# Attention of batches 1 to 3 in three TensorE bursts a job instead of five, and a new order of the banded products

## The chip, the cores and the metric

The kernel runs on one core of a Trainium2 chip. A core has a matrix engine (TensorE, with its own queue), VectorE (DVE), ScalarE (ACT), GpSimd (POOL) and SyncE (SP), which here only issues DMA transfers. Each engine works through its own instructions in order, and semaphores tie the engines together. The metric is the time of one execution on the device, in microseconds (us); a run's time is one execution, and the median of the runs counts.

## The reference

Four batches, 8 heads, 576 positions, head dimension 64. Attention has two branches that are added: one over keys and values that are averaged in groups of four (144 queries by 144 keys, each result repeated four times), and one in which a position sees only the seven positions within three of it. The result goes through two gated feed-forward layers.

```
q_d, k_d, v_d = means of q, k, v over groups of 4 positions
out_up    = repeat(softmax(scale * q_d @ k_d.T) @ v_d, 4)
mask      = abs(pos[:, None] - pos[None, :]) < 4
out_local = softmax(where(mask, scale * q @ k.T, -1e9)) @ v
x = (out_up + out_local), heads side by side: 2304 x 512
x = ((sigmoid(x @ w_gate) * (x @ w_val)) @ w_out)        # 512 -> 1536 -> 512
h = x @ w_in                                              # 512 -> 2048
out = (h * sigmoid(1.702 * h)) @ w_out2                   # 2048 -> 512
```

## The kernel before

**Dense layers.** Every dense product is done in single precision by three passes over a split into high and low halves: high by high, low by high, high by low (L822 to L824, function `passes`). A pass is a 128x128 weight times 512 columns. Hidden values go to the PSUM banks `ph`, results to the banks `acc`. Layer 1 is done batch by batch; a *visit* of a batch is 432 passes. The weights arrive as 64-bit words; ScalarE (L744) and VectorE (L746, L748, L753) turn them into 32-bit numbers, ScalarE makes the high half `whi` (L762), VectorE or GpSimd the low half `wlo` (L764). In the visit of batch 0, when the weights come for the first time, the low halves are VectorE's.

**Attention.** It is cut into 16 jobs: a job is a batch and a pair of heads. The four jobs of batch 0 run before the dense work; those of batch b+1 run within the visit of batch b, in bursts on TensorE between dense passes. A job before has five bursts:

- `scores` (L570): banded scores of 24 query tiles by two heads, on 64x32 parts of the array, into two banks `pa`. VectorE adds the mask (L577), then softmax on VectorE and ScalarE (L585 to L596), and VectorE transposes the probabilities into `tt` (L597).
- `down` (L610): pooled scores of 144 by 144, into two banks. VectorE finds the maxima (L617, L620), ScalarE takes the exponential, VectorE the sum's reciprocal (L632, L633), ScalarE scales: `pd`.
- `down_t` (L654): eight transposes of `pd`, copied by ScalarE into `pdt`.
- `values`, first part: the first half of the banded values (`band(0)`, L682, on 32x64 parts) and the pooled values (L690). ScalarE copies the pooled part to `up`.
- `values`, second part: `band(1)`, again L682.

Then `combine` adds `up` to the bands out of the banks (three reads on VectorE, L711), and ScalarE and VectorE split the sum into the halves `xhi` and `xlo` (L720 for the low half), which are the dense layer's input in the next visit. L507 on VectorE pools the values `vg`; GpSimd pools queries and keys (L538, L540 into `qd`, `kd`).

**Order.** All operations are given to a planner (`Plan`) with an estimated duration, the buffers that they read and write, and a due time; for attention that is a fraction of the job's stretch (`due(x)`). The planner runs through time, gives each engine the ready operation with the smallest due time, and writes the fixed order that each engine then executes. A buffer or bank is held from its first writer to its last reader. Batches 1 to 3 have only two banks (`pas`) for attention, so each burst must wait until the readers of the burst before have let them go; batch 0 has more. At the start, filler products (L1272) stand where TensorE would have nothing to do.

## Time and profile before

| what | value |
|---|---|
| median of 3 runs | 942.98 us (941.73 to 944.8) |
| the profiled execution's own time | 942.11 us |
| its span in the trace | 940.4 us |
| granted TensorE clock, mean of the span | 0.992 |
| TensorE busy | 922.7 us, 98 % |
| TensorE weight loads busy | 761.4 us, 81 % |
| VectorE, ScalarE, GpSimd busy | 685.8, 499.7, 364.2 us |

The profiled execution is one of its own beside the three runs; durations in the trace are its. A share of busy time is an average over stages: attention of batch 0 with the start, the visits of layer 1, then layer 2. TensorE's entries in a timeline carry a modelled end, so one reads their starts: a dense pass is shown with 0.39 us but its successor starts 0.227 us later. A burst is one row with a count of hardware passes (a single-precision product is two of them), and its effect is seen in the starts of the dense passes around it.

### The profile page before, as it was taken

Reading aid. Unit: us, or ns where it says so; the run is one execution under the profiler, and the core shown is the slowest. Engines: PE = TensorE matmul, PEld = TensorE weight load, DVE = VectorE, ACT = ScalarE, POOL = GpSimd, SP = SyncE. Lnnn points to the kernel's source line nnn. Section 1 sums busy time; section 2 is a strip of 40 time slices with the busy share of each in tenths; the row PEclk is TensorE's granted clock in tenths of the full one; section 3 lists DMA queues with packets and bytes.
Section 4 is the critical chain, followed back from the end, with each engine's and each line's share of the span. In section 5 each row is a group of like instructions: output and inputs, shape, how many; then the busy total and the mean of one; then the engine's idle time right before and its main releaser. Section 6 shows DMA issues by size and latency. Waiting matters only on the chain.

```text
span 940.4 us, 19224 instructions
## 1 busy us (share of the span) xinstructions
PE 922.7 (98%) x7515; PEld 761.4 (81%) x7515; DVE 685.8 (73%) x1170; ACT 499.7 (53%) x1080; POOL 364.2 (39%) x337
## 2 busy tenths in 40 slices
PE   6999999999999999999999999999999999999997
PEld 5777777877778778789988888888888788888896
DVE  5799999887767786755565639878897977764364
ACT  3666666455554555555655436545664544554463
POOL 6352202334233442234678423222696222232241
PEclk8899999999999999999999999999999999999999
DMA  9447647463265633220154103011551101043000
GB/s 274 138 152 205 206 136 196 138 175 135 71 177 181 174 127 102 84 75 2 62 184 153 51 0 135 23 45 41 181 166 46 62 24 45 33 149 110 30 16 23
DMA packets 51980, 101.70 MB, mean 108 GB/s; under 512 B 5489, under 2 KB 18619, under 8 KB 51890
## 3 DMA queue, kind: packets, MB, share of 16 engines
q1 hardware_dynamic: 51890, 100.48, 34.4%
q8 instruction: 59, 0.97, 0.4%
q14 instruction: 31, 0.25, 0.1%
HBM read 75.29 MB, written 25.17 MB: 107 GB/s over the span
## 4 chain that ended last, share of the span: by engine, by line
PE 88%; DVE 6%; DMA 2%; ACT 1%; issue 1%; SPq 1%; POOL 0%; ACTq 0%; DVEq 0%
PE ph L822 14%; PE ph L823 13%; PE ph L824 13%; PE acc L822 9%; PE acc L823 9%; PE acc L824 9%; PE pa L822 5%; PE pa L824 5%; PE pa L823 5%; PE pa L682 2%; DMA vt<-v 1%; PE pa L570 1%; DMA vg<-v 1%; PE acc L494 1%; PE pa L690 1%; DVE we L748 1%
## 5 line engine op out<-in xcount | busy, mean ns | idle before, releaser
L764 POOL TENSOR_TENSOR wlo<-w,whi 128x512 fp32r<-128x512 f32 x77 | 104.9, 1362 | 179.9 <-ACT whi L762 177.9
L822 PE MATMUL ph<-xhi,whi 128*128 128x512 f32 (+1 forms) x418 | 166.3, 398 | 0.4 <-ACT th L865 0.4
L824 PE MATMUL ph<-xlo,whi 128*128 128x512 f32 (+1 forms) x418 | 161.5, 386 | 1.4 <-POOL xlo L720 1.4
L823 PE MATMUL ph<-xhi,wlo 128*128 128x512 f32 (+1 forms) x418 | 161.7, 387 | 0.0
L762 ACT CAST whi<-w 128x512 fp32r<-128x512 f32 x159 | 97.9, 619 | 83.5 <-PE ph L824 28.2
L764 POOL TENSOR_TENSOR wlo<-wr,whi 128x512 fp32r<-128x512 f32 x58 | 78.9, 1361 | 142.7 <-ACT whi L762 133.0
L822 PEld LDWEIGHTS ph<-xhi,whi 128*128 128x128 f32 x418 | 78.6, 188 | 19.9 <-issue 4.3
L824 PEld LDWEIGHTS ph<-xlo,whi 128*128 128x128 f32 x418 | 78.7, 188 | 18.3 <-POOL xlo L720 2.2
L823 PEld LDWEIGHTS ph<-xhi,wlo 128*128 128x128 f32 x418 | 78.7, 188 | 14.5 <-DVE wlo L764 0.4
L822 PE MATMUL acc<-ghi,whi 128*128 128x512 f32 (+1 forms) x240 | 90.3, 376 | 0.0
L870 DVE SCALAR_TENSOR_TENSOR th<-th,ph 128x512 f32<-128x512 f32 (+1 forms) x68 | 41.2, 605 | 66.8 <-PE ph L824 59.3
L762 ACT CAST whi<-wr 128x512 fp32r<-128x512 f32 (+1 forms) x115 | 67.1, 587 | 40.3 <-PE ph L824 13.7
L823 PE MATMUL acc<-ghi,wlo 128*128 128x512 f32 (+1 forms) x240 | 88.4, 369 | 0.0
L824 PE MATMUL acc<-glo,whi 128*128 128x512 f32 (+1 forms) x240 | 88.3, 368 | 0.0
L764 DVE TENSOR_TENSOR wlo<-w,whi 128x512 fp32r<-128x512 f32 x82 | 62.8, 766 | 23.3 <-ACT whi L762 23.2
L865 ACT ACTIVATE th<-ph 128x512 f32<-128x512 f32 (+1 forms) x68 | 36.3, 534 | 48.0 <-PE ph L824 48.0
L744 ACT ACTIVATE we<-w 128x512 f32<-128x512 f32 x68 | 45.7, 672 | 19.0 <-DMA w<-w 13.5
L748 DVE SCALAR_TENSOR_TENSOR we<-w,we 128x512 int32<-128x512 int32 x68 | 55.0, 808 | 1.1
L538 POOL TENSOR_TENSOR half<-qt 128x288 f32<-128x288 f32 x16 | 20.2, 1265 | 85.1 <-DMA qt<-qT 84.8
L822 PEld LDWEIGHTS acc<-ghi,whi 128*128 128x128 f32 x240 | 45.2, 189 | 7.9 <-issue 0.6
L824 PEld LDWEIGHTS acc<-glo,whi 128*128 128x128 f32 x240 | 45.3, 189 | 7.6
L874 DVE TENSOR_TENSOR glo<-th,ghi 128x512 fp32r<-128x512 f32 (+1 forms) x60 | 46.5, 776 | 6.6 <-ACT ghi L873 5.8
(254 smaller groups left out, 2289.1 us busy)
## 6 DMA issues: line engine op xcount, KB each, us to landing
w<-w SPq DMA_DIRECT2D x68, 512.0 KB
w<-gd SPq DMA_DIRECT2D x32, 256.0 KB
gd<-w SPq DMA_DIRECT2D x30, 256.0 KB
w2d<-we SPq DMA_DIRECT2D x28, 256.0 KB
qt<-qT SPq DMA_DIRECT2D x16, 288.0 KB
kt<-kT SPq DMA_DIRECT2D x16, 288.0 KB
st<-x2d SPq DMA_DIRECT2D x36, 128.0 KB
x2d<-ev SPq DMA_DIRECT2D x16, 256.0 KB
```

Source lines behind the costliest of these rows:

```text
L538: op("pool", 760.0, lambda: nc.gpsimd.tensor_add(half.t, s[:, :, :, 0], s[:, :, :, 1]), [bsrc], [half], due)
L682: nc.tensor.matmul(s.t[h * D:(h + 1) * D, q:q + NQ], vt.t[ks, g, v0 + h * D:v0 + (h + 1) * D], tt.t[ks, h, g, :NQ], start=True, stop=True, ...
L744: op("act", 617.0, lambda: nc.scalar.activation(e.t.bitcast(F32), words(1, F32), AF.Copy, scale=2.0 ** -112), [w], [e], due)
L748: op("dve", 602.0, lambda: nc.vector.scalar_tensor_tensor(e.t, words(0), 29, e.t, op0=ALU.logical_shift_right, op1=ALU.bitwise_or), [w], [ ...
L762: op("act", act_ns(n), lambda: nc.scalar.copy(vh(), vm()), [rm], [rh], due)
L764: op(eng, ns, lambda: on.tensor_sub(vl(), vm(), vh().bitcast(F32)), [rm, rh], [rl], due)
L822: nc.tensor.matmul(o, lhi, rhi, start=first, stop=False, skip_group_check=more)
L823: nc.tensor.matmul(o, llo, rhi, start=False, stop=False, skip_group_check=more)
L824: nc.tensor.matmul(o, lhi, rlo, start=False, stop=last, skip_group_check=more)
L865: op("act", act_ns(n, True), lambda h=h: nc.scalar.activation(th.t[:, :n], h.t[:, :n], AF.Tanh, scale=0.5 if layer == 1 else 1.702 / 4.0), ...
L870: op("dve", dve_ns(n), lambda: nc.vector.scalar_tensor_tensor(th.t[:, :n], th.t[:, :n], 1.0, hb[-1].t[:, :n], op0=ALU.add, op1=ALU.mult), ...
L874: op("dve", dve_ns(n), lambda: nc.vector.tensor_sub(gl.t[:, :n], th.t[:, :n], gh.t[:, :n].bitcast(F32)), [th, gh], [gl], t)
```

## The change

For batches 1 to 3 a job has three bursts. The first holds the banded scores (now L571) and the pooled scores (L618), in the same two banks, the pooled ones behind the column where the banded ones end. The second holds the first half of the bands (L693) and the transposes (L676). The third holds the second half of the bands (L693) and the pooled values (L716). Second and third share one pair of banks, so that a job takes a pair twice instead of four times. The due times move: pooled scores from 0.5 to 0.1 of the stretch, transposes from 0.65 to 0.5, values from 0.9 to 0.6, combine from 0.9 and 1.0 to 0.6 and 0.7. Batch 0 keeps its bursts. For all batches the loop of a band now has the head outside and the two row quarters inside, so that the quarter, and the bank with it, changes at every product, and the planned durations of the values are smaller.

```diff
--- before.py
+++ after.py
@@ -542,7 +542,7 @@
 
         def front(self):
 
-            return [self.pools, self.scores, self.down]
+            return [self.pools, self.scores, self.down] if self.b == 0 else [self.pools, self.scores]
 
         def back(self):
             return [self.down_t, self.values]
@@ -560,8 +560,9 @@
 
             ss = [bank(self.banks) for _ in range(2)]
             qt, kt, sc, pt, tt, nm, sm = self.qt, self.kt, self.sc, self.pt, self.tt, self.nm, self.sm
-
-            def pe():
+            n = NG * NU
+
+            def scored():
                 for t in range(NT):
                     g, i = divmod(t, 4)
                     t = NG * i + g
@@ -571,12 +572,24 @@
                                          qt.t[hs, NQ * t:NQ * t + 32], kt.t[hs, NQ * t:NQ * t + NU],
                                          start=True, stop=True, tile_position=(h * D, 32 * i))
 
-            n = NG * NU
-            op("pe", 1500.0, pe, [qt, kt], [*ss, (sc, 0), (sc, 1)], self.due(0.1))
+            when = self.due(0.1)
+            if self.b == 0:
+                op("pe", 1500.0, scored, [qt, kt], [*ss, (sc, 0), (sc, 1)], when)
+            else:
+                qd, kd, nmd, smd, pd = self.qd, self.kd, self.nmd, self.smd, self.pd
+
+                def pe():
+                    scored()
+                    self.pooled(ss, n)
+
+                op("pe", 1600.0, pe, [qt, kt, qd, kd],
+                   [*ss, (sc, 0), (sc, 1), nmd, (smd, 0), (smd, 1), (pd, 0), (pd, 1)], when)
             for h in range(2):
                 op("dve", dve_ns(n), lambda h=h: nc.vector.tensor_add(
                     sc.t[:, h], ss[h].t[:, :n].rearrange("p (g c) -> p g c", c=NU), mask),
-                   [ss[h]], [(sc, h)], self.due(0.1))
+                   [ss[h]], [(sc, h)], when)
+            if self.b:
+                self.pooled_softmax(ss, n, when, [(sc, 0), (sc, 1)])
 
             def spread(x):
                 return x.t[:, :, :, None].to_broadcast([P, 2, NG, NU])
@@ -598,31 +611,37 @@
                 out=tt.t.rearrange("p h g c -> p (h g c)"), in_=pt.t.rearrange("p h g c -> p (h g c)")),
                [pt], [tt], at)
 
+        def pooled(self, ss, c):
+            qd, kd = self.qd, self.kd
+            for r in range(2):
+                for h in range(2):
+                    nc.tensor.matmul(ss[h].t[:GH, c + r * G:c + (r + 1) * G],
+                                     qd.t[h * D:(h + 1) * D, r * GH:(r + 1) * GH],
+                                     kd.t[h * D:(h + 1) * D, :], start=True, stop=True)
+
         def down(self):
 
 
             ss = [bank(self.banks) for _ in range(2)]
             qd, kd, nmd, smd, pd = self.qd, self.kd, self.nmd, self.smd, self.pd
-
-            def pe():
-                for r in range(2):
-                    for h in range(2):
-                        nc.tensor.matmul(ss[h].t[:GH, r * G:(r + 1) * G],
-                                         qd.t[h * D:(h + 1) * D, r * GH:(r + 1) * GH],
-                                         kd.t[h * D:(h + 1) * D, :], start=True, stop=True)
-
             at = self.due(0.5)
-            op("pe", 560.0, pe, [qd, kd], [*ss, nmd, (smd, 0), (smd, 1), (pd, 0), (pd, 1)], at)
+            op("pe", 560.0, lambda: self.pooled(ss, 0), [qd, kd],
+               [*ss, nmd, (smd, 0), (smd, 1), (pd, 0), (pd, 1)], at)
+            self.pooled_softmax(ss, 0, at, [])
+
+        def pooled_softmax(self, ss, c, at, masked):
+
+            nmd, smd, pd = self.nmd, self.smd, self.pd
             for h in range(2):
                 op("dve", dve_ns(2 * G), lambda h=h: nc.vector.reduce_max(
-                    nmd.t[:, 2 * h:2 * h + 2], ss[h].t[:GH, :2 * G].rearrange("p (r k) -> p r k", k=G), axis=AX.X),
-                   [ss[h]], [(nmd, h)], at)
-            op("dve", 90.0, lambda: nc.vector.tensor_scalar_mul(nmd.t, nmd.t, -SCALE_D), [], [nmd], at)
+                    nmd.t[:, 2 * h:2 * h + 2], ss[h].t[:GH, c:c + 2 * G].rearrange("p (r k) -> p r k", k=G),
+                    axis=AX.X), [ss[h]], [(nmd, h)], at)
+            op("dve", 90.0, lambda: nc.vector.tensor_scalar_mul(nmd.t, nmd.t, -SCALE_D), masked, [nmd], at)
 
             def ex(h):
                 for r in range(2):
                     x = 2 * h + r
-                    nc.scalar.activation(pd.t[:, h, r], ss[h].t[:GH, r * G:(r + 1) * G], AF.Exp,
+                    nc.scalar.activation(pd.t[:, h, r], ss[h].t[:GH, c + r * G:c + (r + 1) * G], AF.Exp,
                                          bias=nmd.t[:, x:x + 1], scale=SCALE_D, accum_out=smd.t[:, x:x + 1])
 
             for h in range(2):
@@ -643,29 +662,45 @@
 
         def down_t(self):
             self.pdt = buf("pdt")
-            ss = [bank(self.banks) for _ in range(2)]
+            ss = self.ss = [bank(self.banks) for _ in range(2)]
             pd, pdt = self.pd, self.pdt
+            c, due, more = (0, 0.65, []) if self.b == 0 else (HALF // 2, 0.5, [halves[self.b, self.hp // 2].vt, self.tt])
 
             def pe():
+                if self.b:
+                    self.band(0, *ss)
                 for h in range(2):
                     for kh in range(2):
                         for r in range(2):
-                            o = kh * G + r * GH
+                            o = c + kh * G + r * GH
                             nc.tensor.transpose(ss[h].t[:GH, o:o + GH], pd.t[:, h, r, kh * GH:(kh + 1) * GH],
                                                 ident.t[:GH, :GH])
 
-            op("pe", 500.0, pe, [(pd, 0), (pd, 1), ident], [*ss, (pdt, 0), (pdt, 1)], self.due(0.65))
+            op("pe", 500.0 + 500.0 * len(more) / 2, pe, [(pd, 0), (pd, 1), ident, *more],
+               [*ss, (pdt, 0), (pdt, 1)], self.due(due))
             for h in range(2):
                 op("act", 370.0, lambda h=h: nc.scalar.copy(
-                    pdt.t[:, h], ss[h].t[:GH, :2 * G].rearrange("p (k q) -> p k q", q=G)),
-                   [ss[h]], [(pdt, h)], self.due(0.65))
+                    pdt.t[:, h], ss[h].t[:GH, c:c + 2 * G].rearrange("p (k q) -> p k q", q=G)),
+                   [ss[h]], [(pdt, h)], self.due(due))
+
+        def band(self, x, sa, sz):
+
+            vt, tt, v0 = halves[self.b, self.hp // 2].vt, self.tt, self.hp % 2 * P
+            for g in range(NG):
+                for h in range(2):
+                    for s, i in ((sa, x), (sz, 2 + x)):
+                        ks, q = slice(32 * i, 32 * i + NU), NQ * (NG * x + g)
+                        nc.tensor.matmul(s.t[h * D:(h + 1) * D, q:q + NQ],
+                                         vt.t[ks, g, v0 + h * D:v0 + (h + 1) * D], tt.t[ks, h, g, :NQ],
+                                         start=True, stop=True, tile_position=(32 * i, h * D))
 
         def values(self):
 
 
 
             b, hp = self.b, self.hp
-            sa, sz = (bank(self.banks) for _ in range(2))
+            early = self.b > 0
+            sa, sz = self.ss if early else (bank(self.banks) for _ in range(2))
             half = halves[b, hp // 2]
             vd, vt, pdt, tt = half.vd, half.vt, self.pdt, self.tt
             up = self.up = buf("up")
@@ -674,17 +709,8 @@
                 new_x((1, b))
             xh, xl = xs[1, b]
 
-            def band(x):
-                for g in range(NG):
-                    for s, i in ((sa, x), (sz, 2 + x)):
-                        ks, q = slice(32 * i, 32 * i + NU), NQ * (NG * x + g)
-                        for h in range(2):
-                            nc.tensor.matmul(s.t[h * D:(h + 1) * D, q:q + NQ],
-                                             vt.t[ks, g, v0 + h * D:v0 + (h + 1) * D], tt.t[ks, h, g, :NQ],
-                                             start=True, stop=True, tile_position=(32 * i, h * D))
-
             def pe():
-                band(0)
+                self.band(int(early), sa, sz)
                 for kh in range(2):
                     for h in range(2):
                         nc.tensor.matmul(sa.t[h * D:(h + 1) * D, c0:c0 + G],
@@ -693,10 +719,12 @@
 
 
             xfs = [buf("xf") for _ in range(2)]
-            op("pe", 1400.0, pe, [vd, pdt, vt, tt], [sa, sz, up, *xfs], self.due(0.9))
+            at = self.due(0.6 if early else 0.9)
+            op("pe", 1100.0, pe, [vd, pdt, vt, tt], [sa, sz, up, *xfs], at)
             op("act", 260.0, lambda: nc.scalar.activation(up.t, sa.t[:, c0:c0 + G], AF.Copy, scale=0.25),
-               [sa], [up], self.due(0.9))
-            op("pe", 700.0, lambda: band(1), [vt, tt, up], [sa, sz], self.due(0.9))
+               [sa], [up], at)
+            if not early:
+                op("pe", 500.0, lambda: self.band(1, sa, sz), [vt, tt, up], [sa, sz], at)
             for n, s in enumerate((sa, sz)):
                 self.combine(n * HALF, (n + 1) * HALF, s, xfs[n], n == 0, xh, xl)
 
@@ -704,7 +732,7 @@
             b, hp, up = self.b, self.hp, self.up
             hi = min(z, T)
             m = hi - a
-            at = self.due(0.9 if first else 1.0)
+            at = self.due((0.9 if first else 1.0) - (0.3 if b else 0.0))
             part = (hp, first)
 
             def add(out, o0, o1):
```

TensorE, job 0 of batch 2, end of the banded scores (`kt_123`, `qt_121` are its keys and queries, `pa_156` and `pa_157` the two banks, `acc`, `ph` banks of dense passes). Before, two pieces that have 56 dense passes between them:

```order
L570 MATMUL pa_156<-kt_123,qt_121 32x30
L570 MATMUL pa_157<-kt_123,qt_121 32x30
L822 MATMUL acc_151<-ghi_94,whi_79 128x512
L823 MATMUL acc_151<-ghi_94,wlo_83 128x512
L824 MATMUL acc_151<-glo_96,whi_79 128x512
```

```order
L824 MATMUL ph_155<-xlo_92,whi_80 128x512
L610 MATMUL pa_156<-kd_134,qd_132 72x144
L610 MATMUL pa_157<-kd_134,qd_132 72x144
L610 MATMUL pa_156<-kd_134,qd_132 72x144
L610 MATMUL pa_157<-kd_134,qd_132 72x144
L822 MATMUL ph_155<-xhi_90,whi_80 128x512
```

After, one piece:

```order
L571 MATMUL pa_156<-kt_123,qt_121 32x30
L571 MATMUL pa_157<-kt_123,qt_121 32x30
L618 MATMUL pa_156<-kd_134,qd_132 72x144
L618 MATMUL pa_157<-kd_134,qd_132 72x144
L618 MATMUL pa_156<-kd_134,qd_132 72x144
L618 MATMUL pa_157<-kd_134,qd_132 72x144
L850 MATMUL acc_151<-ghi_94,whi_79 128x512
L851 MATMUL acc_151<-ghi_94,wlo_83 128x512
```

The pooled scores moved forward by 60 dense passes, and the two places at which the dense passes were left are one.

TensorE, the same job's transposes (`pd_138` are the pooled probabilities, `tt_128` the banded ones). Before:

```order
L824 MATMUL ph_154<-xlo_92,whi_78 128x512
L654 MATMUL pa_156<-ident,pd_138 72x72 x4
L654 MATMUL pa_157<-ident,pd_138 72x72 x4
L822 MATMUL ph_154<-xhi_90,whi_78 128x512
L823 MATMUL ph_154<-xhi_90,wlo_82 128x512
```

After:

```order
L693 MATMUL pa_156<-tt_128,vt 64x24
L693 MATMUL pa_157<-tt_128,vt 64x24
L676 MATMUL pa_156<-ident,pd_138 72x72 x4
L676 MATMUL pa_157<-ident,pd_138 72x72 x4
L850 MATMUL ph_155<-xhi_90,whi_80 128x512
L851 MATMUL ph_155<-xhi_90,wlo_84 128x512
```

The transposes come 27 dense passes earlier and directly behind the first half of the bands, which itself comes 57 passes earlier than it did.

VectorE, job 1 of batch 1, in the visit of batch 0 (`xf_145`, `xf_146` take the sums out of the two banks; `small`, `pt_126`, `tt_128` belong to the softmax of job 2; `w`, `we`, `wlo` to the dense weights). Before:

```order
L597 STREAM_TRANSPOSE tt_128<-pt_126 128x384
L711 TENSOR_TENSOR xf_145<-pa_156,up_143 128x288
L746 TENSOR_SCALAR we_87<-we_87 128x512
L874 TENSOR_TENSOR glo_95<-th_97,ghi_93 128x512
L720 TENSOR_TENSOR xlo_92<-xf_145,xhi_90 128x288
L748 SCALAR_TENSOR_TENSOR we_87<-w_86,we_87 128x512
L711 TENSOR_TENSOR xf_146<-pa_157,up_143 128x224
L753 SCALAR_TENSOR_TENSOR w_114<-w_86,we_87 128x512
L711 TENSOR_TENSOR tails<-pa_157,up_143 128x64
```

After:

```order
L602 TENSOR_REDUCE small<-pt_126 128x12
L774 TENSOR_SCALAR we_88<-we_88 128x512
L739 TENSOR_TENSOR xf_145<-pa_156,up_143 128x288
L739 TENSOR_TENSOR xf_146<-pa_157,up_143 128x224
L739 TENSOR_TENSOR tails<-pa_157,up_143 128x64
L605 TENSOR_SCALAR small<-small 128x12
L606 RECIPROCAL small<-small 128x12
L748 TENSOR_TENSOR xlo_92<-xf_145,xhi_90 128x288
L609 TENSOR_TENSOR pt_126<-pt_126,small 128x12x30
```

The three reads out of the banks (L711 before, L739 now) stand in one piece instead of between weight conversions, and ahead of the end of the next job's softmax (L605 to L610) instead of behind it.

## Rows read from the trace of the kernel before

**Rows 1.** The page: busy time by engine, and the chain that ended last.

```profile
PE 922.7 (98%) x7515; PEld 761.4 (81%) x7515; DVE 685.8 (73%) x1170; ACT 499.7 (53%) x1080; POOL 364.2 (39%) x337
...
PE 88%; DVE 6%; DMA 2%; ACT 1%; issue 1%; SPq 1%; POOL 0%; ACTq 0%; DVEq 0%
```

**Rows 2.** Windows: us, busy time and count by engine, PEclk, DMA, GB/s.

```profile
100.00:150.00 50.00, 50.00 (x607) 39.67 (x606) 48.07 (x102) 30.41 (x70) 6.03 (x4) 1.00 0.52 160
```

**Rows 3.** Timeline of TensorE, 95 to 130 us: start, us, engine, line, what.

```profile
95.25 0.39 PE L824 MATMUL acc<-glo,whi 128*128 128x512 f32 x1
95.56 0.71 PE L610 MATMUL pa<-kd,qd 64*72 64x144 f32 x8
96.21 0.50 PE L822 MATMUL acc<-ghi,whi 128*128 128x512 f32 x1
96.55 0.40 PE L823 MATMUL acc<-ghi,wlo 128*128 128x512 f32 x1
...
103.59 0.39 PE L824 MATMUL acc<-glo,whi 128*128 128x512 f32 x1
103.82 0.66 PE L654 MATMUL pa<-ident,pd 72*72 72x72 f32 x8
104.29 0.48 PE L822 MATMUL acc<-ghi,whi 128*128 128x512 f32 x1
104.60 0.40 PE L823 MATMUL acc<-ghi,wlo 128*128 128x512 f32 x1
...
106.20 0.39 PE L824 MATMUL ph<-xlo,whi 128*128 128x512 f32 x1
106.52 1.02 PE L570 MATMUL pa<-kt,qt 64*32 64x30 f32 x96
107.47 0.50 PE L822 MATMUL ph<-xhi,whi 128*128 128x512 f32 x1
107.80 0.39 PE L823 MATMUL ph<-xhi,wlo 128*128 128x512 f32 x1
...
113.83 0.39 PE L824 MATMUL ph<-xlo,whi 128*128 128x512 f32 x1
114.14 0.89 PE L682 MATMUL pa<-tt,vt 30*64 30x24 f32 x48
114.97 0.50 PE L822 MATMUL acc<-ghi,whi 128*128 128x512 f32 x1
115.31 0.40 PE L823 MATMUL acc<-ghi,wlo 128*128 128x512 f32 x1
```

**Rows 4.** Weight loads of L682: all (ns min/median/max), and the first of a band.

```profile
L682 PEld LDWEIGHTS pa<-tt,vt x1344: 127/133/222, 24.2 to 405.7; 30*64 30x64 f32 x192
...
111.10 0.15 PEld L682 LDWEIGHTS pa<-tt,vt 30*64 30x64 f32 x4 [0.35 <-DVE sc L586]
```

**Rows 5.** Timeline of TensorE: transposes of batches 2 and 3.

```profile
274.29 1.30 PE L654 MATMUL pa<-ident,pd 72*72 72x72 f32 x8
...
342.08 0.96 PE L654 MATMUL pa<-ident,pd 72*72 72x72 f32 x8
```

**Rows 6.** Timelines of TensorE and VectorE: `wlo` made and used, 156 to 165 us.

```profile
156.67 0.39 PE L822 MATMUL ph<-xhi,whi 128*128 128x512 f32 x1
157.03 0.50 PE L823 MATMUL ph<-xhi,wlo 128*128 128x512 f32 x1
...
162.52 0.69 DVE L764 TENSOR_TENSOR wlo<-w,whi 128x512 fp32r<-128x512 f32 x1
...
164.84 0.39 PE L823 MATMUL acc<-ghi,wlo 128*128 128x512 f32 x1
```

**Rows 7.** Timeline of VectorE, 138 to 175 us: reads out of the banks, combine.

```profile
141.57 0.46 DVE L711 TENSOR_TENSOR xf<-pa,up 128x288 f32<-128x288 f32 x1 [1.08 <-PE pa L682]
...
167.15 0.45 DVE L711 TENSOR_TENSOR xf<-pa,up 128x288 f32<-128x288 f32 x1
...
168.94 0.39 DVE L720 TENSOR_TENSOR xlo<-xf,xhi 128x224 fp32r<-128x224 f32 x1
```

## The prediction

> **What bounds the kernel now.** I read first the busy times of the page: TensorE is busy 98 % of the span, the other engines 81 % (its own weight loads) or less [rows 1]. So what counts is time in which TensorE does something other than stream the dense products of the two layers, and time in which it waits. The chain that ended last says the same: 88 % of it lies on TensorE [rows 1]. Then I read VectorE by stretches, because a share of the whole span hides stages: in the first dense visit it is busy 48.07 of 50 us [rows 2]. There it is a second bound, although it is at 73 % over the whole [rows 1]. Last I read TensorE's timeline around the attention of the next batch. A dense pass (a 128x128 weight by 512 columns) starts every 0.227 us (31 of them from 96.55 to 103.59); attention comes as a burst between two passes, and costs more than its own length, because the pass after it is late too [rows 3].
>
> I price a burst by its excess: the start of the second dense pass after it, less the start of the last dense pass before it, less two passes of 0.227. From [rows 3]: scores L570 107.80 - 106.20 - 0.454 = 1.15; pooled scores L610 96.55 - 95.25 - 0.454 = 0.85; transposes L654 104.60 - 103.59 - 0.454 = 0.56; second half of the banded values L682 115.31 - 113.83 - 0.454 = 1.03. The fifth burst, first half of the banded values with the pooled values, is in the new kernel burst C with the same products, so it drops out. The four sum to 3.59 us a job; batches 1 to 3 have 12 jobs, and these four bursts read the same in each of them, except for the waits named below.
>
> **The change part by part.**
>
> 1. *Pooled scores behind the scores (burst A).* One entry, one way back. Entry 0.32 (106.20 to 106.52), scores 0.95 (to 107.47), pooled scores 0.65 (95.56 to 96.21), second pass late 0.34, less 0.454: 1.80 against 1.15 + 0.85 = 2.00, so -0.20 a job [rows 3].
>
> 2. *Transposes behind the first half of the bands (burst B).* Entry 0.31, bands 0.83 (114.14 to 114.97), transposes 0.47 (103.82 to 104.29), second pass late 0.31, less 0.454: 1.47 against 1.03 + 0.56 = 1.59, so -0.12 a job [rows 3]. What no row shows is a step from a tiled product straight to a transpose. The transposes enter from a dense pass in 0.23 (103.59 to 103.82), the tiled bursts in 0.31 or 0.32: a transpose pays no entry now, and if it pays one after a band, about the 0.10 that a tiled burst pays over a pass, the gain falls to -0.02. Below 1.47 nothing in these rows points, since a dense pass and a band are left and entered once. So a job saves 0.21 to 0.32; I take 0.30, near the top, since the times inside a burst are plain rows. Twelve jobs: **-3.6** (-2.5 to -3.9).
> The Trainium skill, "TensorEngine Tiling (Array Packing)", Key Properties, says that a change of tiling mode drains the engine. The 0.32 against 0.23 agrees; by that rule bands and transposes would still pay it between them, and this term would be -2.5.
>
> 3. *Order of the bands.* Same products, now row quarter by row quarter. I price it at 0: the first four weight loads of a band, 128 ns each, together span 0.15 us, and 48 of 133 ns fit in 0.83 [rows 3, 4]. The four products of a group already run side by side, on two quarters and two column halves; the next group needs the same four places, in either order. Bounds: if it ran at the scores' rate, 0.95 for 96 passes, a band took 0.48 (rival 1); nothing excludes a small loss, but its rows would have to lose their overlap.
>
> 4. *Two waits.* Two transposes of batches 2 and 3 took 1.30 and 0.96 instead of 0.66 [rows 3, 5]: they waited in the middle for the normalized pooled weights, which came late from a crowded VectorE. In the new order the pooled softmax starts some 60 passes earlier, beside the scores, and 48 products of the band stand ahead of the transposes. 0.64 + 0.30: **-0.9** (0 to -1.0). Next to be late there is the transposed `tt`, which the band needs at the same point; in the visits of batches 1 and 2 VectorE has room for it.
>
> 5. *VectorE in the first visit.* The combine's three bank reads (now L739) stand behind burst C in VectorE's queue, in one piece, and the queue is in order. If VectorE gets there first, it stands idle, and queued behind are the next job's softmax and the low halves of weights (`wlo`), for which TensorE waits. Two rows show how thin this is: L823 at 157.03 started 0.36 after its forerunner instead of 0.227, because `wlo` came late; the one made at 162.52 ended 163.21 and is used at 164.84, a lead of 1.63 [rows 6]. One idle of the kind stands in the trace: 1.08, ahead of L711 at 141.57 [rows 7]. And the last job's combine, at 167.15 to 169.33 (first and last of five rows) and thus behind that `wlo`, now comes ahead of it: 2.18 against the lead of 1.63, 0.55 short [rows 7]. I take one more idle of 1.08 and a third to a half of that shortfall, as other work can slide: **+1.3**. Bounds: 0, if VectorE always arrives late; +4, for an idle of 1.08 at three jobs and the whole shortfall. In the two later visits VectorE has slack, and I price the same at 0.
>
> 6. *Fewer bank pairs, earlier pooling, planned times: 0* (-1 to +2). A job takes its two banks twice instead of four times; what hides the hand-over is 6 to 18 dense passes (1.4 to 4.1 us) between bursts, and the three bank reads, of at most 0.46 each [rows 7], take 1.4 at most; where only 6 passes lie between, this cover is the first to fail. GpSimd's pooled `kd` is now needed at the scores; GpSimd is busy 39 % of the span [rows 1], and what it costs if it is late is in the bound. The start of the kernel, with batch 0, keeps its bursts; only its planned times change. SP issues the same transfers.
>
> **Sum** against the profiled execution, 942.11: -3.6 - 0.9 + 1.3 + 0 = -3.2, 938.9. That execution lies 0.87 under the median of the runs (942.98), so **939.8**.
>
> **The rivals.**
>
> *Rival 1, the new band order speeds up the bands.* 24 bands by 0.83 - 0.48 = 0.35: 8.4 less, 931.4. For it: the scores change the row half at each product and run at 9.9 ns a pass, the bands at 17.3 [rows 3]. Against it: the scores use eight places of the array, the bands four, which is the same ratio.
> The Trainium skill, "TensorE: Matmul & The Clock Gate", Part 3, The mechanism, says that a weight load overlaps running matmuls only where the row group differs; by it the old order, two products on one quarter, held loads up, and this rival is its result. The trace speaks against the "only": the four loads of [rows 4] include both column halves of one quarter.
>
> *Rival 2, slower: VectorE idles at every combine of the first visit.* If it arrives early at all four jobs and the idle is twice the 1.08, since both halves' reads now wait for the whole of burst C, that is 8.6, and with 0.55 of the moved combine 9.2 in place of 1.3: 939.8 + 7.9 = 947.7. It decides from the point where the idles together exceed the lead of 1.63 by more than the bursts save. For it: 96 % busy and the order of the queue. Against it: the combine's due time moved earlier with the burst, and an engine that is behind arrives late, not early.
>
> *Rival 3, the bursts don't shorten:* each switch inside a burst costs what entry and exit cost now. 939.8 + 3.6 = 943.4. Against it: entry and exit are measured against dense passes of 128 rows and 512 columns, which don't stand inside a burst.
>
> *Rival 4, VectorE keeps up:* term 5 is 0, 938.5. It lies within the forecast's own range.
>
> **How the numbers follow.** Forecast 0.48 (937.0 to 942.5, time 939.8), rival 4 0.14 (938.5), rival 1 0.12 (931.4), rival 3 0.12 (943.4), rival 2 0.14 (947.7, from about 945). The range 934.0 to 947.0 leaves out rival 1 and the upper half of rival 2, some 0.19. A measurement of this kernel can tell about 0.3 % from no change, 2.8 us: faster is under 940.15, slower over 945.8. Faster: a bit over half of the forecast (0.27), nearly all of rival 4 (0.12), rival 1 (0.12): 0.51. Slower: most of rival 2, 0.13 with a little of rival 3. Same: 0.36.
>
> **What would show it.** In TensorE's timeline L618 directly behind L571 and L676 behind L693, with excess 1.80 for A and 1.47 for B, and transposes of 0.66 throughout (terms 1, 2, 4). Bands of 0.83 (term 3) or 0.48 (rival 1). In the first visit, idle of VectorE ahead of L739 that ends on TensorE, and starts of L851 that come late after `wlo` (term 5, rival 2). I am wrong in the large if batches 2 and 3 show new waits at a bank, or if the first visit ends later by more than 2 us.

## The result, and the profile after

The changed kernel takes 951.15 us (median of 5 runs, 948.27 to 953.53), the kernel before 944.34 in the five runs that stand beside it (941.73 to 946.06). The ratio is 1.0074 with an interval of 1.0046 to 1.0102: some 7 us slower, where 3 us faster was forecast, and outside the range. The profiled execution took 953.53, the longest of the five, with a span of 951.8; its mean granted clock is 0.981.

The page after, in answer to [rows 1]: TensorE has as much to do as before, in a span that is 11 us longer.

```profile
PE 925.9 (97%) x7502; PEld 767.1 (81%) x7502; DVE 683.6 (72%) x1170; ACT 498.9 (52%) x1080; POOL 355.2 (37%) x337
```

TensorE's timeline after, one burst A and one burst B (start, us, engine, line, what), in answer to [rows 3]:

```profile
119.42 0.39 PE L852 MATMUL ph<-xlo,whi 128*128 128x512 f32 x1
119.74 0.89 PE L693 MATMUL pa<-tt,vt 30*64 30x24 f32 x48
120.56 0.69 PE L676 MATMUL pa<-ident,pd 72*72 72x72 f32 x8
121.06 0.47 PE L850 MATMUL ph<-xhi,whi 128*128 128x512 f32 x1
121.37 0.39 PE L851 MATMUL ph<-xhi,wlo 128*128 128x512 f32 x1
...
127.39 0.39 PE L852 MATMUL acc<-glo,whi 128*128 128x512 f32 x1
127.71 1.02 PE L571 MATMUL pa<-kt,qt 64*32 64x30 f32 x96
128.66 0.71 PE L618 MATMUL pa<-kd,qd 64*72 64x144 f32 x8
129.30 0.50 PE L850 MATMUL ph<-xhi,whi 128*128 128x512 f32 x1
129.64 0.40 PE L851 MATMUL ph<-xhi,wlo 128*128 128x512 f32 x1
```

The bursts do what was forecast. A: 129.64 - 127.39 - 0.454 = 1.80. B: 121.37 - 119.42 - 0.454 = 1.50. All eleven bursts A in the three visits read 1.79 to 1.81, and eleven of the twelve bursts B 1.50 or 1.51. So the loss is not there. To find it I cut both executions at four points that are the same dense pass in each: the first pass behind the start (the 25th of all: 24 stand among the attention of batch 0), the first of batch 1's visit, the hundredth pass of layer 1's last stretch (256 columns wide), and the end. Timeline of TensorE before, then after, the passes at the three inner cuts:

```profile
58.43 0.50 PE L822 MATMUL ph<-xhi,whi 128*128 128x512 f32 x1
...
171.10 0.39 PE L822 MATMUL ph<-xhi,whi 128*128 128x512 f32 x1
...
423.58 0.28 PE L824 MATMUL ph<-w,whi 128*128 128x256 f32 x1
```

```profile
67.84 0.78 PE L850 MATMUL ph<-xhi,whi 128*128 128x512 f32 x1
...
184.27 0.39 PE L850 MATMUL ph<-xhi,whi 128*128 128x512 f32 x1
...
432.98 0.28 PE L852 MATMUL ph<-w,whi 128*128 128x256 f32 x1
```

The start is 67.84 against 58.43 us, 9.4 longer; the first visit (of batch 0) 116.43 against 112.67, 3.8 longer; the visits of batches 1 and 2 with the hundred passes 248.71 against 252.48, 3.8 shorter; the rest 518.8 against 516.8. The gain is where it was looked for, and two stages ahead of it lose three to four times as much. The same cuts for every kernel that was run (one profiled execution each; times in us). The ratio is to executions of the kernel before that ran beside that kernel, with medians from 943.67 to 945.74, so it is not the quotient of two medians of this table:

| kernel | start | first visit | visits of batches 1, 2 | rest | median | ratio to before, 95 % |
|---|---|---|---|---|---|---|
| before | 58.43 | 112.67 | 252.48 | 516.8 | 944.34 | |
| changed | 67.84 | 116.43 | 248.71 | 518.8 | 951.15 | 1.0074 (1.0046 to 1.0102) |
| e1_old_planned | 60.30 | 115.90 | 248.70 | 516.9 | 943.60 | 0.9976 (0.9945 to 1.0007) |
| e2_before_new_planned | 65.16 | 115.05 | 252.64 | 516.9 | 949.11 | 1.0038 (1.0008 to 1.0068) |
| e3_band_order | 59.97 | 112.70 | 251.76 | 516.5 | 943.68 | 0.9979 (0.9949 to 1.0009) |
| e4_combine_late | 57.02 | 113.55 | 248.73 | 517.5 | 943.40 | 0.9979 (0.9943 to 1.0014) |
| e5_values_late | 62.48 | 112.65 | 249.48 | 516.8 | 943.13 | 0.9974 (0.9946 to 1.0002) |
| e6_combine_pool | 60.50 | 112.25 | 248.70 | 516.7 | 940.18 | 0.9946 (0.9914 to 0.9978) |
| e7_start_kept_busy | 59.12 | 114.93 | 252.19 | 516.8 | 946.23 | 0.9992 (0.9956 to 1.0029) |
| e8_measured_planned | 60.91 | 110.61 | 255.27 | 516.6 | 946.63 | 1.0006 (0.9972 to 1.0039) |
| e9_after_pool | 64.65 | 115.83 | 248.71 | 517.8 | 947.83 | 1.0039 (1.0010 to 1.0067) |
| e10_measured_batch0 | 59.96 | 109.42 | 248.70 | 517.9 | 940.52 | 0.9956 (0.9925 to 0.9986) |

The start differs by a few us between kernels that have the same order there (57.0 to 62.5 among before, e1, e3, e4, e5 and e6, mean 59.8), so 9.4 is one draw. The three with the changed kernel's planned durations and without added fillers have 64.7 to 67.8, mean 65.9: some 6 us more. The first visit repeats better: before and e3 have one order there and differ by 0.03 us, e2 and e7 by 0.12. Not every profiled execution is a typical one: the changed kernel's lies 2.4 us above its median, e4's and e10's, each the shortest of its kernel, 4.9 and 2.7 below.

### The profile page after: what moved, and what is told of

It reads as the page before. It is cut to its first block, busy times and chain, and to the rows that moved or that the text cites. A ratio compares the mean times of both kernels' runs of the same rounds, so it can differ in the third digit from the quotient of the medians.

```text
span 951.8 us, 19163 instructions
## 1 busy us (share of the span) xinstructions
PE 925.9 (97%) x7502; PEld 767.1 (81%) x7502; DVE 683.6 (72%) x1170; ACT 498.9 (52%) x1080; POOL 355.2 (37%) x337
## 5 line engine op out<-in xcount | busy, mean ns | idle before, releaser
L792 POOL TENSOR_TENSOR wlo<-wr,whi 128x512 fp32r<-128x512 f32 x58 | 81.0, 1396 | 155.3 <-ACT whi L790 146.9
L792 DVE TENSOR_TENSOR wlo<-w,whi 128x512 fp32r<-128x512 f32 x82 | 61.5, 750 | 21.7 <-ACT whi L790 21.7
L893 ACT ACTIVATE th<-ph 128x512 f32<-128x512 f32 (+1 forms) x68 | 36.3, 533 | 66.5 <-PE ph L852 66.5
L774 DVE TENSOR_SCALAR we<-we 128x512 int32<-128x512 int32 x68 | 43.8, 644 | 37.8 <-ACT we L772 37.8
L851 PEld LDWEIGHTS acc<-ghi,wlo 128*128 128x128 f32 x240 | 45.6, 190 | 9.6 <-DVE wlo L792 2.4
L772 ACT ACTIVATE we<-w 128x512 f32<-128x512 f32 x68 | 45.4, 670 | 12.8 <-DMA w<-w 12.8
L776 DVE SCALAR_TENSOR_TENSOR we<-w,we 128x512 int32<-128x512 int32 x68 | 50.3, 740 | 1.1
```

Source lines behind the costliest of these rows:

```text
L772: op("act", 617.0, lambda: nc.scalar.activation(e.t.bitcast(F32), words(1, F32), AF.Copy, scale=2.0 ** -112), [w], [e], due)
L774: op("dve", 335.0, lambda: nc.vector.tensor_scalar(e.t, e.t, 3, None, op0=ALU.logical_shift_left), [], [e], due)
L776: op("dve", 602.0, lambda: nc.vector.scalar_tensor_tensor(e.t, words(0), 29, e.t, op0=ALU.logical_shift_right, op1=ALU.bitwise_or), [w], [ ...
L792: op(eng, ns, lambda: on.tensor_sub(vl(), vm(), vh().bitcast(F32)), [rm, rh], [rl], due)
L851: nc.tensor.matmul(o, llo, rhi, start=False, stop=False, skip_group_check=more)
L893: op("act", act_ns(n, True), lambda h=h: nc.scalar.activation(th.t[:, :n], h.t[:, :n], AF.Tanh, scale=0.5 if layer == 1 else 1.702 / 4.0), ...
```

## The experiments

**e1, the planned durations of batch 0 taken back.** The only thing that the change does to batch 0, beside the order inside a band, is to give the planner smaller durations for the value products.

```diff
-            op("pe", 1100.0, pe, [vd, pdt, vt, tt], [sa, sz, up, *xfs], at)
+            op("pe", 1100.0 if early else 1400.0, pe, [vd, pdt, vt, tt], [sa, sz, up, *xfs], at)
...
-                op("pe", 500.0, lambda: self.band(1, sa, sz), [vt, tt, up], [sa, sz], at)
+                op("pe", 700.0, lambda: self.band(1, sa, sz), [vt, tt, up], [sa, sz], at)
```

> The changed kernel with one thing taken back: in batch 0 the planned durations of the two value products are 1400 and 700 ns again, as in the kernel before (batches 1 to 3 keep 1100). Theory S (the loss is made at the start: the smaller planned durations make the planner write another order for batch 0, whose chain then ends some 9 us later): the first dense pass behind the start comes back from 67.8 to 58.4 us (within 2), and the time falls by about 9 to 940-943. Theory V (the loss is made by VectorE in the first visit, and the late start is given back later): the time stays at 948-952.

Measured: 943.6 us, just above the 940 to 943 of theory S, and start 60.3. Theory S holds for the start. The first visit stays long, 115.9, so V was right that something is lost there too; it is not the aftermath of a late start.

**e2, the same two numbers in the kernel before, alone.**

```diff
-            op("pe", 1400.0, pe, [vd, pdt, vt, tt], [sa, sz, up, *xfs], self.due(0.9))
+            op("pe", 1400.0 if b else 1100.0, pe, [vd, pdt, vt, tt], [sa, sz, up, *xfs], self.due(0.9))
...
-            op("pe", 700.0, lambda: band(1), [vt, tt, up], [sa, sz], self.due(0.9))
+            op("pe", 700.0 if b else 500.0, lambda: band(1), [vt, tt, up], [sa, sz], self.due(0.9))
```

> The kernel before with one thing of the change alone: the two planned durations of batch 0 (1400 to 1100, 700 to 500 ns). Products, bursts and due times are untouched. Theory S: the first dense pass behind the start moves from 58.4 to about 67, and the time rises by 7 to 10 us to 951-954. Theory V: no change, 943-946.

Measured: 949.11 us, start 65.2. Two numbers that no instruction carries make the kernel before slower by 0.38 %, theory S's direction, and about half of its size. What they change is the order. In these lines S is banded scores, P pooled scores, T transposes, V first bands with pooled values, B second bands, each with its job, F dense passes; they begin behind the second pooling of values (L494) and its transposes:

```
before    S3 V1 T2 B1 P3 F  S(next) V2 F B2 F F P(next) T3 F F V3 B3
e2        F S3 V1 P3 T2 B1 V2 F B2 F T3 F S(next) V3 F B3 F P(next)
```

P3 moved ahead of T2 and B1, and so V2 needs two banks that P3 has just written. The timelines of the changed kernel, which has this order too (with P(next) behind S(next), in burst A), show the chain (VectorE, ScalarE, TensorE):

```profile
43.70 0.46 DVE L739 TENSOR_TENSOR xf<-pa,up 128x288 f32<-128x288 f32 x1 [2.54 <-PE acc L693]
...
44.85 0.67 DVE L639 TENSOR_SCALAR smalld<-smalld 72x4 f32<-72x4 f32 x1
...
45.55 0.38 ACT L644 ACTIVATE pd<-pa,smalld 72x144 f32<-72x144 f32 x1 [0.65 <-DVE smalld L639]
...
46.43 1.49 PE L693 MATMUL pa<-tt,vt 30*64 30x24 f32 x48 [2.85 <-ACT pd L644]
```

VectorE, in order, waits 2.54 us for B1 and only behind the combine of job 1 scales the maxima of P3 (L639). ScalarE waits for those, then reads P3's banks (L644). TensorE waits 2.85 for the banks.

The changed kernel's start has one more wait, near its end, which e2 has only in small (0.40 at 63.43), and passes at 0.43 us behind it:

```profile
65.51 0.63 PE L852 MATMUL ph<-xlo,whi 128*128 128x512 f32 x1 [2.23 <-POOL xlo L748]
65.94 0.63 PE L850 MATMUL ph<-xhi,whi 128*128 128x512 f32 x1
```

GpSimd's low half comes late there. From V2 to the first pass behind the start the changed kernel takes 21.4 us (46.43 to 67.84), e2 19.15 (46.01 to 65.16). e9, which has the changed kernel's planned durations too, shows the same wait of 2.23 us, e1 without them 0.64. What makes it was not tested by itself.

**e3, the new order inside a band, alone.**

```diff
                 for g in range(NG):
-                    for s, i in ((sa, x), (sz, 2 + x)):
...
-                        for h in range(2):
+                    for h in range(2):
+                        for s, i in ((sa, x), (sz, 2 + x)):
```

> The kernel before with the new order inside a band alone (head outside, row quarters inside), planned durations as before. Both theories: a band stays at 0.83 us from its first product to the next dense pass, the time within 2 us of before. The rival of the prediction (bands of 0.48) would give about 8 us less.

Measured: 943.68 us, no difference that can be told. TensorE's timeline of e3, one second half of a band:

```profile
89.61 0.39 PE L824 MATMUL ph<-xlo,whi 128*128 128x512 f32 x1
89.92 0.89 PE L682 MATMUL pa<-tt,vt 30*64 30x24 f32 x48
90.75 0.50 PE L822 MATMUL ph<-xhi,whi 128*128 128x512 f32 x1
```

90.75 - 89.92 = 0.83, as before the change. Rival 1 is out.

**e7, the new order of the start with TensorE kept busy.** e2's order again, with filler products in front of the two instructions that waited.

```diff
+    NW1, NW2 = 16, 36
...
                 for h in range(2):
+                    if h and self.b == 0 and self.hp == 2:
+                        self.warmer(NW1)
...
+        def warmer(self, n):
+            for _ in range(n):
+                nc.tensor.matmul(accs[3].t[:, :WARM_N], warm, warm[:, :WARM_N], start=True, stop=True)
...
             def pe():
+                if b == 0 and hp == 2:
+                    self.warmer(NW2)
                 band(0)
...
```

> e2_before_new_planned with 52 filler products more on TensorE (bf16, 128 columns, into a bank that nobody reads): 16 ahead of the second half of the transposes of job 2 of batch 0, where TensorE waited 1.14 us, and 36 ahead of that job's first bands, where it waited 2.82. The order of all else is that of e2. Theory C (most of what the new order of the start costs is the clock: after the two waits TensorE runs at half its speed from 43 to 56 us with 9.7 us of work in a row): with the engine kept busy the clock stays at 1.00 there, the first dense pass behind the start comes 4 to 5 us earlier than in e2 (60 to 61.5 instead of 65.2), and the time falls from 949 to 944-945. Theory D (the waits themselves and the chain through ScalarE and VectorE cost it, the slow work is hidden behind them): less than 1.5 us of change, 948-950.

The waits of e2 on TensorE, and its windows from 46 to 56 us (us, then busy time and count of TensorE, its weight loads, VectorE, ScalarE and GpSimd, the granted clock, DMA share, GB/s):

```profile
41.61 0.44 PE L654 MATMUL acc<-ident,pd 72*72 72x72 f32 x4 [1.14 <-ACT pdt L659]
46.01 1.49 PE L682 MATMUL pa<-tt,vt 30*64 30x24 f32 x48 [2.82 <-ACT pd L625]
```

```profile
46.00:56.00 10.00, 9.99 (x155) 7.60 (x156) 6.23 (x13) 5.43 (x17) 3.13 (x3) 0.50 0.20 59
```

The same of e7, where 36 fillers stand ahead of the second wait:

```profile
41.13 2.19 PE L668 MATMUL acc<-warm 128*128 128x128 bf16 x36
44.03 0.89 PE L689 MATMUL pa<-tt,vt 30*64 30x24 f32 x48 [0.72 <-ACT pd L626]
```

```profile
46.00:56.00 10.00, 9.79 (x290) 7.47 (x290) 8.98 (x18) 6.55 (x16) 3.95 (x3) 1.00 0.31 98
```

In e2 TensorE works for ten microseconds without a pause and gets 155 instructions done at a granted clock of 0.50 (1.2 GHz); in e7 290 at 1.00. The same work, from V2 to the first dense pass behind the start, takes 19.15 us in e2 and 15.09 in e7 (44.03 to 59.12), with the order untouched: 4.1 less. That pass comes at 59.1 instead of 65.2, against 60 to 61.5 expected, but 1.3 of these 6 us are not the fillers' work: e7's execution was ahead by that much before the first of them (T2 begins at 38.72, in e2 at 40.06). By the ratios to before (1.0038 and 0.9992) the time falls by 0.46 %, 4.3 us, as the 4.1 would have it, though the two intervals overlap. That is theory C: most of what e2's order of the start costs is not the 4 us of waiting but the slow clock behind it. What is left of e2's loss lies in its first visit (114.9 against 112.7), in which all bursts are those of the kernel before.

**e4 and e5, dues of batch 1 taken back**, on top of e1: in e4 of the combine alone, in e5 of the value bursts as well.

```diff
-            at = self.due((0.9 if first else 1.0) - (0.3 if b else 0.0))
+            at = self.due((0.9 if first else 1.0) - (0.3 if b > 1 else 0.0))
```

```diff
-            c, due, more = (0, 0.65, []) if self.b == 0 else (HALF // 2, 0.5, [halves[self.b, self.hp // 2].vt, self.tt])
+            c, due, more = (0, 0.65, []) if self.b == 0 else (HALF // 2, 0.5 if self.b > 1 else 0.65, [halves[self.b, self.hp // 2].vt, self.tt])
...
-            at = self.due(0.6 if early else 0.9)
+            at = self.due(0.6 if b > 1 else 0.9)
```

> e1_old_planned with the due times of the combine of batch 1 as before (0.9 and 1.0 of the stretch, not 0.6 and 0.7); everything else stays. Theory P (the place of the combine in VectorE's queue costs the first visit its gain: ahead of the low halves of weights that TensorE needs at the visit's end): the waits of 1.24 and 1.05 us at L850 and L851 near the 410th pass and the ten passes at half clock behind them go; the first visit (from the first dense pass behind the start to the first of batch 2's visit) falls from 115.9 to 111.5-112.5 us, the time by 3 to 4. Theory W (VectorE's total work bounds that visit, wherever the combine stands): the visit stays at 113 us or more and waits for VectorE come at another place.

> e1_old_planned with all due times of second and third burst and of the combine of batch 1 as before (0.65, 0.9, 0.9 and 1.0): the last burst of batch 1 then stands at the same dense pass as in the kernel before (404 of 432), not 57 passes ahead. Theory P: as the run before, 111.5-112.5 us for the first visit. Theory W: 112.7 us or more, no shorter than before, since bursts spread over the whole visit give VectorE the same time as before.

The end of the first visit in e1, TensorE's timeline:

```profile
167.16 0.39 PE L852 MATMUL ph<-xlo,whi 128*128 128x512 f32 x1
168.63 0.50 PE L850 MATMUL acc<-ghi,whi 128*128 128x512 f32 x1 [1.08 <-ACT whi L790]
169.91 0.52 PE L851 MATMUL acc<-ghi,wlo 128*128 128x512 f32 x1 [0.78 <-DVE wlo L792]
170.25 0.60 PE L852 MATMUL acc<-glo,whi 128*128 128x512 f32 x1
170.65 0.63 PE L850 MATMUL acc<-ghi,whi 128*128 128x512 f32 x1
171.08 0.63 PE L851 MATMUL acc<-ghi,wlo 128*128 128x512 f32 x1
171.51 0.63 PE L852 MATMUL acc<-glo,whi 128*128 128x512 f32 x1
```

Two halves of weights come late, 2.3 us together, and the nine dense passes behind them start every 0.34 to 0.43 us instead of every 0.227: 1.7 more. Both experiments take this place away. The first visit is 113.55 in e4, where TensorE now waits for the banded probabilities in another place (timeline of TensorE), and 112.65 in e5.

```profile
149.11 0.39 PE L852 MATMUL ph<-xlo,whi 128*128 128x512 f32 x1
151.15 0.89 PE L693 MATMUL pa<-tt,vt 30*64 30x24 f32 x48 [1.65 <-DVE tt L610]
```

Theory P's 111.5 to 112.5 was met by neither; theory W's answer, that the wait turns up elsewhere, fits e4, and e5 lies at its edge. Medians of 943.4 and 943.1 cannot be told from e1, so what this place is worth is read from single traces and not from the runs.

**e6, the combine's low halves of batch 1 on GpSimd**, on top of e1.

```diff
-            eng, ns, on = ("pool", pool_ns(m), nc.gpsimd) if b == 0 else ("dve", dve_ns(m), nc.vector)
+            eng, ns, on = ("pool", pool_ns(m), nc.gpsimd) if b <= 1 else ("dve", dve_ns(m), nc.vector)
```

> e1_old_planned with the low halves of the combine of batch 1 (L748) on GpSimd, as in batch 0, not on VectorE: 4 jobs by about 0.84 us less work on VectorE in the first visit, order of bursts nearly the same. Theory W: the first visit falls by 2 to 4 us from 115.9. Theory P: the wait near the 410th pass shrinks only by what is taken out ahead of it in the last job, about 0.8 us, and the half clock may go with it: 113 to 115.5 us.

Measured: first visit 112.25, 3.65 less than e1, as W said and P did not. The time is 940.18, ratio 0.9946 (0.9914 to 0.9978): 0.5 % faster than the kernel before, and faster than the changed one; from e1 (0.9945 to 1.0007) the runs do not part it. But the way is not W's. Windows of the first visit, e1 and then e6:

```profile
60.30:176.20 115.90, 113.48 (x1169) 90.83 (x1169) 110.18 (x216) 66.12 (x146) 19.51 (x18) 0.99 0.59 167
```

```profile
60.50:172.75 112.25, 111.59 (x1170) 89.75 (x1169) 110.25 (x207) 66.22 (x146) 26.08 (x27) 1.00 0.60 173
```

VectorE has nine instructions fewer, 207 for 216, and is busy just as long, 110.25 for 110.18 us: the others took longer (the 128x512 ones 98.0 us for 147, in e1 95.4 for 148). What went is the late place at the visit's end and the slow clock behind it (0.99 against 1.00).

**e9, the same edit on the changed kernel as it is.**

```diff
-            eng, ns, on = ("pool", pool_ns(m), nc.gpsimd) if b == 0 else ("dve", dve_ns(m), nc.vector)
+            eng, ns, on = ("pool", pool_ns(m), nc.gpsimd) if b <= 1 else ("dve", dve_ns(m), nc.vector)
```

> The changed kernel as it is, with the low halves of the combine of batch 1 on GpSimd alone added (as e6 against e1). Start as in the changed kernel (65 to 68 us at the first dense pass behind it), first visit 112 to 113.5 instead of 116.4 us, time 946.5-948.5 against 951.15. If the first visit's loss in the changed kernel is only the aftermath of the late start, the visit does not move and the time stays above 950.

The time is within what was expected, 947.83, but not for the reason: the first visit is 115.83, not 112 to 113.5, and the start was an early one. Behind the changed kernel's start the edit moves the visit by 0.6 us only; VectorE has ten instructions fewer in it, 211 for 221, and again the same busy time (111.95 for 111.82 us). The visit's length must hang on what the start leaves behind too, as in e2 and e7, whose bursts in it are those of before; how is not shown.

**e8 and e10, planned durations as measured**, on top of e6. If too short durations made the order bad, true ones should make it good.

```diff
-                op("pe", 1500.0, scored, [qt, kt], [*ss, (sc, 0), (sc, 1)], when)
+                op("pe", 1150.0, scored, [qt, kt], [*ss, (sc, 0), (sc, 1)], when)
...
-                op("pe", 1600.0, pe, [qt, kt, qd, kd],
+                op("pe", 1800.0, pe, [qt, kt, qd, kd],
...
-            op("pe", 560.0, lambda: self.pooled(ss, 0), [qd, kd],
+            op("pe", 850.0, lambda: self.pooled(ss, 0), [qd, kd],
...
-            op("pe", 500.0 + 500.0 * len(more) / 2, pe, [(pd, 0), (pd, 1), ident, *more],
+            op("pe", 560.0 + 930.0 * len(more) / 2, pe, [(pd, 0), (pd, 1), ident, *more],
...
-            op("pe", 1100.0 if early else 1400.0, pe, [vd, pdt, vt, tt], [sa, sz, up, *xfs], at)
+            op("pe", 1670.0, pe, [vd, pdt, vt, tt], [sa, sz, up, *xfs], at)
...
-                op("pe", 700.0, lambda: self.band(1, sa, sz), [vt, tt, up], [sa, sz], at)
+                op("pe", 1030.0, lambda: self.band(1, sa, sz), [vt, tt, up], [sa, sz], at)
```

> e6_combine_pool with the planner's durations of all attention products on TensorE at what the traces show with entry and way back: scores 1150, pooled scores 850, transposes 560, bands with pooled values 1670, bands 1030, bursts A 1800 and B 1490 ns. If the start was made slow by planned durations that are too short, true ones should give a start no slower than 60 us and a time of 938-941, as e6 or below. If the order that comes out is a matter of chance and not of true durations, the start can land anywhere from 57 to 68 and the time between 937 and 948.

Measured: 946.63, not 938 to 941. The start (60.9) is as good as with the old durations, not better, and the first visit is 110.6; but the visits of batches 1 and 2 lose 6.6 us to e6, most of it at one pass that waited 2.4 us for ScalarE and the passes at half clock behind it. e10 puts the measured durations on batch 0 alone:

> e8_measured_planned with the measured planned durations for batch 0 alone; the bursts of batches 1 to 3 have those of e6 again (A 1600, B 1000, C 1100). If the 6 us that e8 lost in the visit of batch 2 against e6 came from the longer planned bursts, that visit falls from 122.8 to 116.8 us, start (60.9) and first visit (110.6) stay as in e8, and the time is 935-940. If they came from somewhere else (a transfer that was late by chance, or the order that batch 0 leaves behind), the visit stays near 122 us and the time at 945-947.

Measured: 940.52, ratio 0.9956 (0.9925 to 0.9986), visits of batches 1 and 2 back at 248.7, first visit 109.42, the shortest of all. That the longer planned bursts made e8's wait is likely, since these are all that differs. In e8's trace TensorE waits for an activation (L893, at 324.00) that stands in ScalarE's queue behind a step of the weights (L772, at 323.44), and this waited 2.09 us for their DMA; why the transfer was late is not known. e10 is no faster than e6 by its runs. Windows of the first visit, before and then e10:

```profile
58.43:171.10 112.67, 112.31 (x1172) 89.62 (x1169) 109.66 (x219) 68.77 (x158) 30.06 (x19) 1.00 0.61 176
```

```profile
59.96:169.39 109.43, 109.43 (x1117) 88.69 (x1114) 106.38 (x204) 65.99 (x145) 33.07 (x25) 1.00 0.61 175
```

In both, VectorE is busy for all but 3 us of the visit, and the visit is shorter by what VectorE has less to do in it: 3.3 us of work, 3.2 us of time. But TensorE has less to do there as well: in e8 and e10 the first burst B of batch 1, 1.5 us, stands ahead of the cut, in the start. So this pair does not tell the two engines apart.

## Why the prediction was wrong, step by step

**Bursts (terms 1 and 2): right.** A 1.80 for 1.80, B 1.50 for 1.47. Inside B the transposes follow the band after 0.82 us (119.74 to 120.56) and take 0.50 (to 121.06) for 0.47, so the step from tiled products to transposes costs about 0.03, not the 0.10 of the lower bound. 12 jobs by 0.29 are 3.5 us for the 3.6 forecast. One reading was too smooth: before the change not all bursts of a kind read the same, since scores at 78.31 read 1.58 for a wait behind them.

**Order of the bands (term 3): right**, by e3 and by 0.82 in the changed kernel. (Rival 1's sum left out the eight bands of batch 0, which have the new order too.)

**Two waits (term 4): right.** The visits of batches 1 and 2 gain 3.8 us (e1 the same); eight jobs at 0.30 and the 0.9 of the waits are 3.3. By the traces the bursts of these visits together cost 43.1 us before and 39.8 after, 3.4 less; the 0.4 that is left lies in the passes between them. Why the longer of the two waits was there was misread. It was not a crowded VectorE: ahead of the reciprocals (L633, at 273.55) VectorE's queue stood still for a transfer of values (timeline of VectorE before):

```profile
272.21 1.22 DVE L507 TENSOR_TENSOR vg<-vg 72x1024 f32<-72x1024 f32 x1 [2.16 <-DMA vg<-v]
```

**VectorE in the first visit (term 5): the place was right, the size wrong.** The bursts in it should have gained 1.2, so a term of +1.3 meant a visit as long as before. In e1, behind the start of before, it is 3.2 longer: the term is 4.4, above the upper end of +4. In the changed kernel it is 3.8 longer, 5.0, but that holds what the new start adds. Two things were missing. The clock: the sum priced the wait and nothing behind it, and in e1 1.7 of 4.0 us come after TensorE has got its weights. And the idle of VectorE, on which most of the term was built, is not where it came from: in e1 VectorE never waits at L739, it is late because it is busy. Timelines of the changed kernel at that place (TensorE, VectorE, GpSimd), in answer to [rows 6, 7]:

```profile
174.94 0.39 PE L850 MATMUL acc<-ghi,whi 128*128 128x512 f32 x1
177.33 0.50 PE L851 MATMUL acc<-ghi,wlo 128*128 128x512 f32 x1 [2.00 <-DVE wlo L792]
```

```profile
164.39 0.45 DVE L739 TENSOR_TENSOR xf<-pa,up 128x288 f32<-128x288 f32 x1
...
170.55 0.38 DVE L748 TENSOR_TENSOR xlo<-xf,xhi 128x224 fp32r<-128x224 f32 x1
...
173.09 1.78 DVE L776 SCALAR_TENSOR_TENSOR we<-w,we 128x512 int32<-128x512 int32 x1
174.91 0.69 DVE L781 SCALAR_TENSOR_TENSOR w<-w,we 128x512 int32<-128x512 int32 x1
175.52 1.75 DVE L792 TENSOR_TENSOR wlo<-w,whi 128x512 fp32r<-128x512 f32 x1
```

```profile
172.70 1.62 POOL L792 TENSOR_TENSOR wlo<-wr,whi 128x512 fp32r<-128x512 f32 x1 [4.96 <-ACT whi L790]
174.91 1.81 POOL L792 TENSOR_TENSOR wlo<-wr,whi 128x512 fp32r<-128x512 f32 x1 [0.58 <-ACT whi L790]
```

The last combine (five instructions from 164.39 to 170.93) does stand ahead of that low half now, as forecast, and uses up the lead. Of the last three instructions two, the low half itself among them, take 1.78 and 1.75 us instead of 0.69, while GpSimd splits weights of its own. Such slow instructions stood at this place before the change too (timeline of VectorE before); the low half made there was not one of them:

```profile
159.76 1.78 DVE L753 SCALAR_TENSOR_TENSOR w<-w,we 128x512 int32<-128x512 int32 x1
...
163.13 1.77 DVE L753 SCALAR_TENSOR_TENSOR w<-w,we 128x512 int32<-128x512 int32 x1
```

**The start (term 6): wrong, and the failed step that decided the sign.** The step reads "The start of the kernel, with batch 0, keeps its bursts; only its planned times change", priced 0, with +2 as the upper end. Planned times are what writes the order, and the order of the start was changed by them: P3 ahead of T2 and B1. What the runs showed in place of the 0: two waits of 1.2 and 2.85 us in the start and a granted clock of 0.50 behind them (e2, e7), and in the changed kernel a third wait of 2.23. e2 shows that these two numbers cost 0.38 %, 3.6 us (0.8 to 6.4), by themselves, e1 that without them the changed kernel takes 943.6 and not 951.15; the two differ in size, so some of the loss probably needs the rest of the change as well. The new order could have been read in the code's own plan; none of the rows lies in the start, since those of [rows 2] begin behind it.

**The sum.** Start +6 (mean of three against six executions), first visit +3.8, visits of batches 1 and 2 -3.8: +6, and 6.8 was measured. (The rest, 2.0 longer in the changed kernel's trace, is within 1.1 of before in all others; it is not explained.) Rival 2, the one that ended on the slower side, named the right engine and visit, but a mechanism that did not happen; what made the kernel slower was in none of the rivals.

**What stays open.** Why the first visit is long behind the new start even with the bursts of before (115.05 and 114.93 in e2 and e7) was not settled by an experiment. The traces show more work for VectorE in it: the start has got through 108 of its instructions there instead of 114, so that the visit holds 225 and 113.1 us, against 219 and 109.7 before. Window of the first visit, e2:

```profile
65.16:180.21 115.05, 113.33 (x1169) 89.72 (x1170) 113.12 (x225) 70.08 (x160) 16.68 (x19) 1.00 0.62 177
```

A VectorE that is busy nearly throughout fits all of these runs; that its order, and not its load, makes the difference between e1 and e6, which have the same load, is only argued.

## What to carry to other kernels

A planned duration is not documentation: where a planner writes the order, each number it is given is an edit of every stage that it plans, and the order of those stages has to be read before they are priced at nothing. Price a wait of TensorE together with the passes behind it, because the clock that it loses there can cost more than the wait; where such a wait can't be avoided, filler products ahead of it gave back some 4 us in e7. In a stage where a second engine is busy 97 % of the time, time saved on the first one is not a gain until that engine has less to do or its last work is out of the way.

## What the runs showed of the hardware

In e2 TensorE waited 1.14 and 2.82 us, ahead of 41.61 and 46.01. Its granted clock was 1.00 from 40 to 42 us, 0.69 from 42 to 43, and 0.50 (1.2 GHz) from there through the ten microseconds of work behind the second wait; with fillers in the same places it was 1.00 there. Behind waits of 1.08 and 0.78 in e1 the passes started every 0.40 to 0.43 us instead of every 0.227, up to 173.6.

A VectorE instruction with two inputs in SBUF, 0.69 us by itself, took 1.78 and 1.75 in the rows above where one of GpSimd's splits of weights was already running when it began (172.70 ahead of 173.09, 174.91 ahead of 175.52); L781, which began together with the second of them, took its 0.69. So work that is moved to GpSimd can come back in part on VectorE, which fits e6: nine instructions fewer and the same busy time. The Trainium skill, "SBUF — State Buffer", Who interferes with whom, says that such an instruction and GpSimd's reads contend for one pair of ports; the rows agree.

Four products on two row quarters and two column halves run side by side in either order: a band took 0.83 us with the quarter changing at every second product and at every product (e3). The Trainium skill, "TensorE: Matmul & The Clock Gate", Part 3, The mechanism, lets weight loads overlap running products only where the row group differs, by which the new order should have been the faster one (rival 1); here the order made no difference.
